# A transformer layer on one core: even paces for the MLP's filler products, and its readouts split between ScalarE and GpSimd

## Chip, cores and metric

The kernel runs on one core of one Trainium2 chip. The metric is the time of one execution on the device in microseconds (us); lower is better.

## What is computed

One layer in which attention and a dense MLP run in parallel on the same normalized input, in fp32 (2048 tokens, width 512, 32 heads of 16, 1792 hidden columns):

```python
xn = _layernorm(x, axis=-1)
return x + _A_ref(xn, A_wqkv, A_wo) + _B_ref(xn, B_w1, B_b1, B_w2, B_b2)

# _A_ref: q, k, v of xn @ wqkv, 32 heads
scores = jnp.einsum("bhqd,bhkd->bhqk", q, k) * (Dh ** -0.5)
p = _softmax(scores, axis=-1)
o = jnp.einsum("bhqk,bhkd->bhqd", p, v)        # then @ wo
# _B_ref
h = _gelu(jnp.einsum("bsd,df->bsf", x, w1) + b1)
return jnp.einsum("bsf,fd->bsd", h, w2) + b2
```

## The kernel before

**The sweep.** Attention is a sweep of 512 *units*. Four heads and 512 queries make a tile of 16 units; there are 32 tiles. In a unit TensorE makes four *S* products (scores laid out by query, into banks pS), of which VectorE takes the maxima (L259, `mt`); and, for the unit 20 earlier, four *E* products (scores laid out by key, with the maximum taken off, into banks pT), of which ScalarE makes the exponentials (L304, `pe`). Two *V* halves then multiply the exponentials by the values into the bank pV; they are in fp32, and TensorE makes each of them in two passes.

TensorE's array is used as two groups of 64 rows by four groups of 32 columns, so each product is four instructions (L169), one for each column group, and two products run side by side where one has the upper and one the lower rows. A unit has two halves, `a` = 0 and 1. In each *half unit* stand two S and two E products, then a V half on one row group, and beside it, on the other row group, the *filler* D.

**The filler.** `dense` puts products of the MLP (and of the projections, before and after it) beside the V half. They come from a list of `Group`s, each with one bank pD. A *first-layer group* (`hidden_group`) has 12 products for each row group and gives 128 hidden columns of 512 tokens; there are 56. A *second-layer group* (`sum_group`) has 21 products for each row group and gives 128 tokens; there are 32. How many products a half unit takes is the group's `pace`: a pair of which odd and even units take turns. Both kinds have (3, 4), projections (4, 4). Since a group ends only with a unit, a first-layer group takes 4 units (3, 4, 3 and 2 products a half unit) and a second-layer group 6 (3, 4, 3, 4, 3, 4). First-layer groups stand three, two and two between the second-layer groups of the block of tokens before.

**Readouts.** At the end of a group's last unit ScalarE reads its bank. For a first-layer group that is `hh` (L1005): an Identity with a scale and a bias that are columns, one number for each partition. From the next unit on GpSimd makes hh's cubic for the gelu (L983 to L985), then ScalarE the tanh (L972, `t`), then GpSimd the rest (L977 to L980, result `g`, which the second layer reads). For a second-layer group it is `yt` (L1031): a copy with a scale that is a column; GpSimd adds it to the running sum (L1033). Once in 16 units ScalarE also reads pV (L330, `osb`), and VectorE makes three small operations for the maxima (L270, L280, L281) and a reciprocal (L348).

**Order.** The order on each engine is the order in which the program is written: `unit` writes a unit, `later(n, ...)` puts a step n units on, `pooled` puts steps on GpSimd's list, which takes some 2500 ns of them a unit. pD and pT share four banks in turn: while a group holds one, the E products have three.

Of the kernel before, what the change touches and what calls it, by code (L numbers as in the profile page):

```python
# [10 lines left out]
I32 = mybir.dt.int32  # L11
# [36 lines left out]
def layer_kernel(ctx: ExitStack, tc: tile.TileContext, x, wqkv, wo, w1, b1, w2, b2, out):  # L48
# [110 lines left out]
    def given(engine, ns):  # L159
        backlog[engine] += ns  # L160
# [37 lines left out]
            product(user, dst[j:j + 32], lhs[:, j:j + 32], rhs, start=start, stop=stop)  # L198


    scale_reg, held = nc.scalar.alloc_register("exp_scale"), [None]

    def exp_scale(m):

        if held[0] != m:
            nc.scalar.reg_load(scale_reg, sexp[0:1, m:m + 1].bitcast(I32))
            held[0] = m
        return scale_reg

    mt_of, ptiles, pv_of = {}, {}, {}  # L210
    queue, slot = [], [0]
# [13 lines left out]
    def pooled(*todo):  # L225
        steps.extend(todo)
# [66 lines left out]
    def e_half(u, n):  # L293

        p, a = divmod(n, 2)
        t, kt = divmod(u, 16)
        g, qb = divmod(t, NQB)
        st = banks("T")
        r = slice(64 * a, 64 * a + 64)
        k0 = (kt % 4) * P  # L300
        tiled(None, st, kst[g % 2][p][kt // 4][r, k0:k0 + P], qst[g % 2][p][qb][r, :], True, True)
        pe = work.tile([P, QB], F32, name="pe", bufs=12)
        ptiles[u, n] = pe
        nc.scalar.activation(pe, st, AF.Exp, scale=exp_scale(g // 2))  # L304
        given("act", 470)

    def v_half(u, a):
# [107 lines left out]
    class Group:  # L415
# [3 lines left out]
        def __init__(self, prods, alloc, finish, ready=None, first=True, last=True, upper=None, pace=FAST):  # L419
            self.prods = prods, prods if upper is None else upper  # L420
            self.alloc, self.finish, self.ready = alloc, finish, ready
            self.first, self.last, self.pace = first, last, pace
            self.n, self.at, self.bank, self.key = [len(p) for p in self.prods], [0, 0], None, None

        def left(self, side=0):
            return self.n[side] - self.at[side]
# [1 line left out]
        def usable(self, side=0):  # L428
            return self.left(side) > 0 and (self.ready is None or self.ready(self.at[side]))

        def product(self, side):

            if self.bank is None:
                self.bank, self.key = self.alloc()
            lhs, rhs = self.prods[side % 2][self.at[side % 2]]()
            start = self.first and self.at == [0, 0]
            if side == 2:
                self.at = [min(self.at[0] + 1, n) for n in self.n]
                nc.tensor.matmul(self.bank, lhs, rhs, start=start, stop=self.last and self.over())  # L439
# [139 lines left out]
    def dense(gen, side):  # L579

        f = group(gen)
        for _ in range(0 if f is None else (f.pace if pos[0] <= NU + 1 else LATE)[pos[0] % 2]):
            if not f.usable(side):
                return
            f.product(side)

    def land():

# [373 lines left out]
    def mlp():  # L962
# [5 lines left out]
        def gelu(hh, g, b, f):  # L968
            t1 = m2.tile([P, QB], F32, name="t1", bufs=2)

            def tanh():
                nc.scalar.activation(t1, t1, AF.Tanh, scale=GELU_C * GELU_A)  # L972
                given("act", 600)
                later(1, rest, True)

            def rest():
                pooled((690, lambda: nc.gpsimd.tensor_scalar(t1, t1, 1.0, gs[:, 1:2], op0=ALU.add, op1=ALU.mult)),  # L977
                       (1280, lambda: nc.gpsimd.tensor_tensor(t1, t1, hh, op=ALU.mult)),  # L978
                       (620, lambda: nc.gpsimd.tensor_scalar(g[:, 0, f, :], t1, 1.0, 0.0, op0=ALU.mult, op1=ALU.add)),
                       (1160, lambda: nc.gpsimd.tensor_tensor(g[:, 1, f, :], t1, g[:, 0, f, :], op=ALU.subtract)),  # L980
                       (0, lambda: done.add((b, f))))
# [13 lines left out]
        def hidden_group(s, f):  # L995
# [6 lines left out]
            def hidden(hp):  # L1002
                hh = m2.tile([P, QB], F32, name="hh", bufs=3)
                scale, bias = fac1[0][:, k // 2:k // 2 + 1], b1_s[:, k:k + 1]
                nc.scalar.activation(hh, hp, AF.Identity, bias=bias, scale=scale)  # L1005
                given("act", 700)
                later(1, lambda: gelu(hh, g, s, f), True)

            return Group([lambda c=c, i=i, j=j: (wc[:, i, c, :], xb[:, j, c, :]) for c in range(NC) for i, j in PAIRS],
                         dbank, hidden, pace=MEAN)  # L1010

        def sum_group(s, q):
            b, t, g = s // 2, s // 2 * 4 + q, gts[s]
# [14 lines left out]

            def store(yp):
                yt = m2.tile([P, D], F32, name="yt", bufs=2)  # L1030
                nc.scalar.activation(yt, yp, AF.Copy, scale=gs[:, 2:3])  # L1031
# [159 lines left out]
```

## Time and profile before

| | |
|---|---|
| time, median of 3 runs | 1552.85 us (1550.26 to 1552.85) |
| the profiled execution | 1555.34 us, of which 1553.6 us are the span of its instructions |
| TensorE's granted clock, mean of the span | 0.993 of full speed; 1.00 from 600 to 1400 us |
| the sweep's middle | 600 to 1400 us: the MLP's groups follow one another without a pause |

In the page, PE is TensorE's matmuls, PEld its weight loads, DVE VectorE, ACT ScalarE, POOL GpSimd. A row of the groups gives line, engine and operation, written tile <- read tiles, shapes, count, then busy us, mean ns of one, and the idle time ahead with what ended it. ScalarE's operations overlap their neighbours a little, so the time for which one keeps the engine is read from its start to the start of the next.

### The profile page before, as it was taken

To read this page: it belongs to the slowest core of one execution; us is meant where nothing else is said; L and a number is where in the kernel's file an instruction comes from. 1 tells how busy PE (TensorE), PEld (TensorE's weight loads), DVE (VectorE), ACT (ScalarE), POOL (GpSimd) and SP (SyncE) were. 2 spreads that over 40 slices of the span, in tenths; PEclk is the share of its full clock that TensorE was granted. 3 is DMA by queue.
4 is the path that set the end of the run, shared out by engine and by line. 5 is a ranking of instruction groups with operands and counts; after the bars stand their busy time and mean duration, and the time that the engine had idled before them with its cause. 6 is when DMAs were issued, how large, how long until landed. Compare 5 with 4: busy or idle time off the path is not lost.

```text
span 1553.6 us, 86338 instructions
## 1 busy us (share of the span) xinstructions
PE 1514.5 (97%) x39203; PEld 806.0 (52%) x39203; DVE 1401.0 (90%) x2372; ACT 1251.6 (81%) x2326; POOL 674.6 (43%) x694
## 2 busy tenths in 40 slices
PE   8998999999999999999999999999999999999997
PEld 4434545555555555555555555555555555555443
DVE  7898989999999999999999999999999999999612
ACT  4316878889888888888888888888888888888771
POOL 3113697546465444435443443555254454521000
PEclk9999999999999999999999999999999999999997
DMA  6454576542111311121112111121112111022412
GB/s 210 124 158 142 167 231 197 180 120 88 50 35 47 91 33 34 36 75 42 35 56 65 46 35 35 35 80 55 36 42 60 45 35 35 22 66 60 150 50 86
DMA packets 113671, 123.72 MB, mean 80 GB/s; under 512 B 24988, under 2 KB 85276, under 8 KB 113304
## 3 DMA queue, kind: packets, MB, share of 16 engines
q1 hardware_dynamic: 113304, 118.21, 25.4%
q8 instruction: 306, 5.01, 1.4%
q14 instruction: 61, 0.50, 0.1%
HBM read 80.61 MB, written 37.34 MB: 76 GB/s over the span
## 4 chain that ended last, share of the span: by engine, by line
PE 84%; DVE 8%; ACT 2%; issue 2%; DMA 2%; SPq 1%; POOL 0%; ACTq 0%; POOLq 0%
PE pV L169 25%; PE pS L169 19%; PE pD L169 19%; PE pT L169 17%; DVE mt L259 6%; PE pT L439 1%; PE pS L439 1%; ACT pe L304 1%; ACT t L972 1%; DVE amx L667 1%; PE pT L532 1%; PE pD L439 1%; DMA ac<-acc_d 0%; PE pV L532 0%; SPq L1064 0%
## 5 line engine op out<-in xcount | busy, mean ns | idle before, releaser
L259 DVE TENSOR_REDUCE mt<-pS 128x1 f32<-128x512 f32 x2048 | 1299.9, 684 | 60.7 <-PE pS L169 43.1
L304 ACT ACTIVATE pe<-pT 128x512 f32<-128x512 f32 x2048 | 1100.0, 598 | 169.5 <-PE pS L169 72.3
L169 PE MATMUL pV<-pe,vv 64*32 64x512 f32 x8192 | 1077.6, 595 | 0.2
L169 PE MATMUL pT<-qst,kst 64*32 64x512 f16 x8192 | 708.2, 378 | 10.4 <-ACT pe L304 8.9
L169 PE MATMUL pS<-kst,qst 62*32 62x512 f16 x8192 | 636.8, 378 | 9.3 <-DVE mt L259 6.0
L169 PEld LDWEIGHTS <-qst 62*32 62x32 f16 x8192 | 271.1, 92 | 226.8 <-issue 77.9
L169 PEld LDWEIGHTS <-kst 64*32 64x32 f16 x8192 | 270.2, 91 | 213.7 <-issue 109.5
L169 PE MATMUL pD<-xb,wc 64*32 64x512 f16 x5376 | 370.5, 377 | 0.0
L169 PE MATMUL pD<-w_s,g 64*32 64x512 f16 x5376 | 359.4, 377 | 0.0
L169 PEld LDWEIGHTS pV<-pe,vv 64*32 64x32 f32 x8192 | 181.5, 105 | 111.2 <-PE pV L169 18.0
L983 POOL TENSOR_TENSOR t<-hh 128x512 f32<-128x512 f32 x56 | 58.3, 1042 | 341.2 <-ACT hh L1005 341.2
L169 PEld LDWEIGHTS <-g 64*32 64x32 f16 x5376 | 113.8, 92 | 38.6
L169 PE MATMUL pD<-xt,wqk_h 64*32 64x512 f16 x1920 | 127.6, 377 | 3.5 <-issue 3.5
L169 PEld LDWEIGHTS <-wc 64*32 64x32 f16 x5376 | 112.6, 91 | 31.1
L360 POOL TENSOR_TENSOR osb<-osb,rb 128x512 f32<-128x512 f32 x31 | 39.9, 1287 | 128.1 <-DMA rb<-den_d 95.1
L1033 POOL TENSOR_TENSOR xa<-xa,yt 128x512 f32<-128x512 f32 x32 | 41.0, 1280 | 119.0 <-ACT yt L1031 119.0
L1070 DVE SCALAR_TENSOR_TENSOR ac<-pS,gs,ac 128x512 f32<-128x512 f32 x20 | 15.0, 751 | 67.0 <-PE pT L169 46.9
L978 POOL TENSOR_TENSOR t<-t,hh 128x512 f32<-128x512 f32 x56 | 71.8, 1283 | 4.7
L985 POOL TENSOR_TENSOR t<-t,hh 128x512 f32<-128x512 f32 x56 | 71.7, 1280 | 4.7
L980 POOL TENSOR_TENSOR g<-t,g 128x512 f16<-128x512 f32 x56 | 65.3, 1166 | 4.7
L977 POOL TENSOR_SCALAR t<-t,gs 128x512 f32<-128x512 f32 x56 | 38.8, 693 | 55.5 <-ACT t L972 55.5
L169 PE MATMUL pS<-wo_s,oc 64*32 64x512 f16 x1008 | 61.7, 378 | 0.3
(139 smaller groups left out, 881.1 us busy)
## 6 DMA issues: line engine op xcount, KB each, us to landing
wch<-in_B_w_dram SPq DMA_DIRECT2D x28, 512.0 KB
wc<-w_d SPq DMA_DIRECT2D x56, 256.0 KB
qk_d<-stg SPq DMA_DIRECT2D x32, 256.0 KB
rb<-den_d SPq DMA_DIRECT2D x124, 64.0 KB
w_d<-wsp SPq DMA_DIRECT2D x28, 256.0 KB
kst<-qk_d SPq DMA_DIRECT2D x128, 48.0 KB
qst<-qk_d SPq DMA_DIRECT2D x128, 48.0 KB
xs<-in_A_x_dram SPq DMA_DIRECT2D x16, 256.0 KB
```

The costliest lines, as they stand in the source:

```text
L169: p = nc.tensor.matmul(*args, **kw)
L259: nc.vector.reduce_max(mt_of[t][:, n, qt, kb:kb + 1], s, axis=AX.X)
L304: nc.scalar.activation(pe, st, AF.Exp, scale=exp_scale(g // 2))
L360: pooled((1280, lambda: nc.gpsimd.tensor_tensor(osb, osb, rb, op=ALU.mult)), (620, lambda: nc.gpsimd.tensor_scalar(ot[:, 0], osb, 1.0, 0.0 ...
L439: nc.tensor.matmul(self.bank, lhs, rhs, start=start, stop=self.last and self.over())
L532: nc.tensor.matmul(pj, xt[:, i, c, t * P:(t + 1) * P], wh[j][:, c, :], start=(n == 0), stop=(n == 11))
L977: pooled((690, lambda: nc.gpsimd.tensor_scalar(t1, t1, 1.0, gs[:, 1:2], op0=ALU.add, op1=ALU.mult)), (1280, lambda: nc.gpsimd.tensor_tenso ...
L978: (1280, lambda: nc.gpsimd.tensor_tensor(t1, t1, hh, op=ALU.mult)),
L980: (1160, lambda: nc.gpsimd.tensor_tensor(g[:, 1, f, :], t1, g[:, 0, f, :], op=ALU.subtract)),
L983: pooled((1040, lambda: nc.gpsimd.tensor_tensor(t1, hh, hh, op=ALU.mult)), (620, lambda: nc.gpsimd.tensor_scalar(t1, t1, 1.0, 1.0 / GELU_A ...
L985: (1280, lambda: nc.gpsimd.tensor_tensor(t1, t1, hh, op=ALU.mult)),
L1033: add = lambda: nc.gpsimd.tensor_tensor(xa, xa, yt, op=ALU.add)
```

## The change

It has four parts.

1. A group counts in half products: `pace` is now a number of halves for each half unit, FAST (8, 8), MEAN (7, 7), SLOW (6, 6). First-layer groups go from MEAN to SLOW, three products in every half unit. Second-layer groups keep MEAN, now three and a half in every half unit; the half product is the product's first or last 256 of 512 columns (`part`), four instructions of their own with weights loaded again.
2. `hh` is read by a plain Copy; the scale and the bias move to a GpSimd step one unit later, ahead of the cubic.
3. `yt` takes its scale from a register that is loaded once, not from a column.
4. A tanh that is due when no group is open, or when 8 or fewer products of the open group are left (both row groups together), is put off by one unit.

ScalarE's order at the same place of the sweep, where two first-layer groups end one after the other (hh is a first-layer readout, t a tanh, pe an exponential, four of them a unit, yt a second-layer readout). Before:

```order
L1005 ACTIVATE hh<-pD,b_s,fac_2410 128x512
L304 ACTIVATE pe<-pT 128x512 x16
L1005 ACTIVATE hh<-pD,b_s,fac_2410 128x512
L972 ACTIVATE t_13028<-t_13028 128x512
L304 ACTIVATE pe<-pT 128x512 x16
L972 ACTIVATE t_13382<-t_13382 128x512
L304 ACTIVATE pe<-pT 128x512 x4
```

and after:

```order
L1016 ACTIVATE hh<-pD 128x512
L305 ACTIVATE pe<-pT 128x512 x16
L1016 ACTIVATE hh<-pD 128x512
L305 ACTIVATE pe<-pT 128x512 x4
L983 ACTIVATE t_13088<-t_13088 128x512
L305 ACTIVATE pe<-pT 128x512 x12
L983 ACTIVATE t_13451<-t_13451 128x512
L305 ACTIVATE pe<-pT 128x512 x4
```

The first tanh has moved from directly behind the second hh to four exponentials, one unit, later; the other one has kept its place.

TensorE's order in the first half unit of three and a half products of a second-layer group (w_s and g are the second layer's operands; the next rows are S and E products). Before, three products, each four pairs of a load and a matmul:

```order
L169 MATMUL pV<-pe,vv 32x512 x4
L169 LDWEIGHTS g
L169 MATMUL pD<-w_s,g 32x512
...
L169 LDWEIGHTS qst_1_2_111
L169 MATMUL pS<-kst_1_1_94,qst_1_2_111 32x512
```

and after, with four pairs more between the last whole product and the S product:

```order
L169 MATMUL pV<-pe,vv 32x512 x4
L169 LDWEIGHTS g
L169 MATMUL pD<-w_s,g 32x512
...
L169 LDWEIGHTS g
L169 MATMUL pD<-w_s,g 32x256
...
L169 LDWEIGHTS qst_1_2_111
L169 MATMUL pS<-kst_1_1_94,qst_1_2_111 32x512
```

TensorE has 64,224 rows in its order after and 62,688 before: 192 products (32 groups, two row groups, three each) are made in two parts.

GpSimd's order where the MLP's first chains begin. Before:

```order
L983 TENSOR_TENSOR t_8171<-hh 128x512
L984 TENSOR_SCALAR t_8171<-t_8171 128x512
L985 TENSOR_TENSOR t_8171<-t_8171,hh 128x512
L983 TENSOR_TENSOR t_8536<-hh 128x512
L984 TENSOR_SCALAR t_8536<-t_8536 128x512
L985 TENSOR_TENSOR t_8536<-t_8536,hh 128x512
L977 TENSOR_SCALAR t_8171<-t_8171,gs 128x512
```

and after:

```order
L1018 TENSOR_SCALAR hh<-hh,fac_2410,b_s 128x512
L994 TENSOR_TENSOR t_8172<-hh 128x512
L995 TENSOR_SCALAR t_8172<-t_8172 128x512
L996 TENSOR_TENSOR t_8172<-t_8172,hh 128x512
L1018 TENSOR_SCALAR hh<-hh,fac_2410,b_s 128x512
L994 TENSOR_TENSOR t_8538<-hh 128x512
L995 TENSOR_SCALAR t_8538<-t_8538 128x512
L996 TENSOR_TENSOR t_8538<-t_8538,hh 128x512
L988 TENSOR_SCALAR t_8172<-t_8172,gs 128x512
```

One step stands ahead of each cubic; the rest of the order is the same.

The diff, without the lines that only carry the new register or the new counters:

```diff
-FAST, MEAN, SLOW, LATE = (4, 4), (3, 4), (3, 3), (6, 6)
+FAST, MEAN, SLOW, LATE = (8, 8), (7, 7), (6, 6), (12, 12)
...
-        def product(self, side):
+        def product(self, side, parts=2):
...
             r = slice(64 * side, 64 * side + 64)
-            self.at[side] += 1
-            tiled("D", self.bank, lhs[r], rhs[r], start, self.last and self.over())
+            done = self.part[side]
+            n = min(parts, 2 - done)
+            cols = slice(done * QB // 2, (done + n) * QB // 2)
+            self.part[side] = (done + n) % 2
+            self.at[side] += (done + n) // 2
+            assert not start or n == 2
+            tiled("D", self.bank[:, cols], lhs[r], rhs[r][:, cols], start, self.last and self.over())
+            return n
...
-        for _ in range(0 if f is None else (f.pace if pos[0] <= NU + 1 else LATE)[pos[0] % 2]):
-            if not f.usable(side):
-                return
-            f.product(side)
+        n = 0 if f is None else (f.pace if pos[0] <= NU + 1 else LATE)[pos[0] % 2]
+        while n > 0 and f.usable(side):
+            n -= f.product(side, n)
...
-            def tanh():
+            def tanh(again=1):
+                if again and (cur[0] is None or cur[0].left(0) + cur[0].left(1) <= 8):
+                    later(1, lambda: tanh(0), True)
+                    return
                 nc.scalar.activation(t1, t1, AF.Tanh, scale=GELU_C * GELU_A)
...
-                nc.scalar.activation(hh, hp, AF.Identity, bias=bias, scale=scale)
-                given("act", 700)
-                later(1, lambda: gelu(hh, g, s, f), True)
+                nc.scalar.activation(hh, hp, AF.Copy)
+                given("act", 600)
+                later(1, lambda: pooled((690, lambda: nc.gpsimd.tensor_scalar(hh, hh, scale, bias, op0=ALU.mult, op1=ALU.add)),
+                                        (0, lambda: gelu(hh, g, s, f))), True)
...
-                         dbank, hidden, pace=MEAN)
+                         dbank, hidden, pace=SLOW)
...
-                nc.scalar.activation(yt, yp, AF.Copy, scale=gs[:, 2:3])
+                nc.scalar.activation(yt, yp, AF.Copy, scale=factor(sum_scale, gs[0:1, 2:3]))
```

More of the change, by code (lines that the diff above doesn't have):

```diff
@@ L198, in tiled, with factor @@
             product(user, dst[j:j + 32], lhs[:, j:j + 32], rhs, start=start, stop=stop)
[L201 to L208, printed above, removed]
+    exp_scale, sum_scale = (nc.scalar.alloc_register(n) for n in ("exp_scale", "sum_scale"))
+    held = {}
+    def factor(reg, src):
+        if held.get(reg.name) != str(src):
+            nc.scalar.reg_load(reg, src.bitcast(I32))
+            held[reg.name] = str(src)
+        return reg
     mt_of, ptiles, pv_of = {}, {}, {}
@@ L303, in e_half @@
         ptiles[u, n] = pe
-        nc.scalar.activation(pe, st, AF.Exp, scale=exp_scale(g // 2))
+        nc.scalar.activation(pe, st, AF.Exp, scale=factor(exp_scale, sexp[0:1, g // 2:g // 2 + 1]))
         given("act", 470)
```

8 lines of the change are left out of this document (5 added, 3 removed).

## Prediction

> **What bounds the kernel now.** I read the page first: busy time and the chain of waits, then the groups of instructions by shape.
>
> ```profile
> PE 1514.5 (97%) x39203; PEld 806.0 (52%) x39203; DVE 1401.0 (90%) x2372; ACT 1251.6 (81%) x2326; POOL 674.6 (43%) x694
> ...
> PE 84%; DVE 8%; ACT 2%; issue 2%; DMA 2%; SPq 1%; POOL 0%; ACTq 0%; POOLq 0%
> PE pV L169 25%; PE pS L169 19%; PE pD L169 19%; PE pT L169 17%; DVE mt L259 6%; PE pT L439 1%; PE pS L439 1%; ACT pe L304 1%; ACT t L972 1%; DVE amx L667 1%; PE pT L532 1%; PE pD L439 1%; DMA ac<-acc_d 0%; PE pV L532 0%; SPq L1064 0%
> ```
> ```profile
> 600.00:1400.00 800.00, 793.85 (x22220) 436.39 (x22212) 772.21 (x1273) 707.70 (x1319) 364.46 (x366) 1.00 0.16 46
> ```
> ```profile
> L304 ACT ACTIVATE pe<-pT 128x512 f32<-128x512 f32 x2048 | 1100.0, 598 | 169.5 <-PE pS L169 72.3 <-PE pT L169 70.3
> L1005 ACT ACTIVATE hh<-pD,b_s,fac 128x512 f32<-128x512 f32 x56 | 43.6, 778 | 3.9
> L506 ACT ACTIVATE pf<-pD 128x512 f32<-128x512 f32 x21 | 12.6, 599 | 10.9 <-PE pS L126 3.8 <-PE pS L169 3.1 <-PE pD L169 2.3
> ```
>
> TensorE is busy 97% of the span and 794 of the 800 us from 600 to 1400, and the chain runs over it for 84%; but VectorE has 772 of those 800 us and ScalarE 708. "Busy" therefore doesn't say what a unit of the sweep costs. For that I took the timelines of single engines and measured from one readout of the MLP's bank to the next. In a timeline each row is start (us), time (us), engine and operation, the count of merged instructions, and in brackets the idle time before. First ScalarE:
>
> ```profile
> 630.04 0.69 ACT L1031 ACTIVATE yt<-pD,gs 128x512 f32<-128x512 f32 x1
> ...
> 640.41 0.78 ACT L1005 ACTIVATE hh<-pD,b_s,fac 128x512 f32<-128x512 f32 x1
> 641.09 2.05 ACT L304 ACTIVATE pe<-pT 128x512 f32<-128x512 f32 x4
> ...
> 650.93 0.78 ACT L1005 ACTIVATE hh<-pD,b_s,fac 128x512 f32<-128x512 f32 x1
> 651.61 0.62 ACT L972 ACTIVATE t<-t 128x512 f32<-128x512 f32 x1
> 652.12 2.05 ACT L304 ACTIVATE pe<-pT 128x512 f32<-128x512 f32 x4
> ...
> 663.20 0.60 ACT L330 ACTIVATE osb<-pV 128x512 f32<-128x512 f32 x1
> 663.69 1.09 ACT L304 ACTIVATE pe<-pT 128x512 f32<-128x512 f32 x2
> ...
> 667.33 0.69 ACT L1031 ACTIVATE yt<-pD,gs 128x512 f32<-128x512 f32 x1
> 667.92 2.05 ACT L304 ACTIVATE pe<-pT 128x512 f32<-128x512 f32 x4
> ...
> 683.03 0.69 ACT L1031 ACTIVATE yt<-pD,gs 128x512 f32<-128x512 f32 x1
> ```
> ```profile
> 1121.83 0.78 ACT L1005 ACTIVATE hh<-pD,b_s,fac 128x512 f32<-128x512 f32 x1
> ...
> 1132.80 0.78 ACT L1005 ACTIVATE hh<-pD,b_s,fac 128x512 f32<-128x512 f32 x1
> ```
> ```profile
> 752.41 0.78 ACT L1005 ACTIVATE hh<-pD,b_s,fac 128x512 f32<-128x512 f32 x1
> 753.09 0.62 ACT L972 ACTIVATE t<-t 128x512 f32<-128x512 f32 x1
> ...
> 768.71 0.69 ACT L1031 ACTIVATE yt<-pD,gs 128x512 f32<-128x512 f32 x1
> ```
>
> A first-layer group lasts 4 units, a second-layer group 6, so the same 4 units take 10.37 us after a yt (630.04 to 640.41), 10.52 us after an hh (640.41 to 650.93) and 10.97 us after an hh with a tanh behind it (1121.83 to 1132.80). The same 6 units take 15.70 us after a yt (667.33 to 683.03) and 16.30 after hh and tanh (752.41 to 768.71). What differs is only how long ScalarE is kept from the next exponential: 0.59 us (667.33 to 667.92), 0.68 (640.41 to 641.09) and 1.19 (650.93 to 652.12). So each 0.1 us more of readout costs about 0.1 us of the program. The mechanism is seen at one such place, on all engines:
>
> ```profile
> 614.32 0.62 ACT L972 ACTIVATE t<-t 128x512 f32<-128x512 f32 x1
> ...
> 614.84 1.56 ACT L304 ACTIVATE pe<-pT 128x512 f32<-128x512 f32 x3
> 615.48 0.40 PE L169 MATMUL pT<-qst,kst 64*32 64x512 f16 x4 [0.39 <-ACT pe L304]
> ```
>
> The exponential that should free a bank of the scores begins at 614.84, and TensorE's next score product stands idle before 615.48 until that one is done. TensorE works in order there, so everything behind waits too.
>
> The second thing is the filler. TensorE's timeline in a second-layer group (each half unit has V's first pass, D's products, V's second pass, and the score products, left out here):
>
> ```profile
> 672.69 0.62 PE L169 MATMUL pV<-pe,vv 64*32 64x512 f32 x4
> 672.71 0.61 PE L169 MATMUL pD<-w_s,g 64*32 64x512 f16 x8
> 673.13 0.61 PE L169 MATMUL pV<-pe,vv 64*32 64x512 f32 x4
> 673.15 0.39 PE L169 MATMUL pD<-w_s,g 64*32 64x512 f16 x4
> ...
> 673.96 0.62 PE L169 MATMUL pV<-pe,vv 64*32 64x512 f32 x4
> ...
> 675.23 0.63 PE L169 MATMUL pV<-pe,vv 64*32 64x512 f32 x4
> 675.27 0.61 PE L169 MATMUL pD<-w_s,g 64*32 64x512 f16 x8
> 675.71 0.60 PE L169 MATMUL pD<-w_s,g 64*32 64x512 f16 x8
> ...
> 676.58 0.60 PE L169 MATMUL pV<-pe,vv 64*32 64x512 f32 x4
> ...
> 677.88 0.62 PE L169 MATMUL pV<-pe,vv 64*32 64x512 f32 x4
> ```
>
> From V to V, a half unit with three D products (8 + 4 instructions from 672.71) takes 1.27 us, and so does the next; with four (8 + 8 from 675.27) it takes 1.35 and then 1.30 (675.23, 676.58, 677.88). A unit of threes is 2.54 us, a unit of fours 2.65. With three, D's row group is free long before V's two passes (0.44 us apart) are, so V sets the length; with four, D and V end together and D sets it.
>
> **The change part by part.**
>
> (1) *Readouts.* hh loses its two per-partition operands, yt its one. Copies of the same shape without any take 0.599 us (pf), an exponential with its scale in a register 0.598 us. An osb, also such a copy, keeps ScalarE for 0.49 us (663.20 to 663.69). So I take 0.50 us in place of 0.68 and 0.59. The 56 scale-and-bias steps go to GpSimd, nearest row:
>
> ```profile
> L977 POOL TENSOR_SCALAR t<-t,gs 128x512 f32<-128x512 f32 x56 | 38.8, 693 | 55.5 <-ACT t L972 55.5
> ```
>
> at 0.7 us each that is 39 us on an engine with 364 busy us in 800. The chain behind hh grows by that step, and the second layer's products wait for its end; but the order has the same products in the same half units in both kernels, and a group's chain has four units for some 7 us of work. So I cost it at nothing; were the cover gone, it would be at most these 39 us. The register load for yt comes once.
>
> (2) *Tanh apart from hh.* Before, 27 of the 56 tanhs stand directly behind an hh; in the changed order one does, and the others stand four exponentials later. A tanh alone keeps ScalarE 0.51 us (651.61 to 652.12).
>
> (3) *What a readout costs.* 6 units of the second layer are by themselves 3 x 2.54 + 3 x 2.65 = 15.57 us, so behind a yt (0.59 us) 15.70 - 15.57 = 0.13 us is lost and behind hh and tanh (1.19 us) 16.30 - 15.57 = 0.73. The two agree: what exceeds 0.46 us is paid in full. By this an hh should cost 0.22 and its 4 units 0.09 more than behind a yt; they take 0.15 more. With 0.50 and 0.51 us, a readout then costs 0.04 and a lone tanh 0.05. Bounds: nothing, and the 0.13 of a yt for each.
>
> (4) *Paces.* First layer: 3, 4, 3, 2 products a half unit become 3, 3, 3, 3. The 4 units were 10.37 - 0.13 = 10.24 us by themselves and become 4 x 2.54 = 10.16; the short last unit had made good for the long second one, so little is gained. Second layer: 3, 3, 4, 4 become three and a half throughout. That is not in the trace. It lies between 2.54 us a unit (V still sets it) and 2.65 (it is as dear as four). In the rows above D is 0.216 us a product (a column group's stream restarts after that time; 675.27 to 675.71 holds two), so three and a half are 0.76 us against V's 2 x 0.44: V sets it, and I take 2.54. The half products are 256 columns wide, about 0.108 us, and the load of the next weights has to hide beneath:
>
> ```profile
> L169 PEld LDWEIGHTS <-g 64*32 64x32 f16 x5376 | 113.8, 92 | 38.6
> ```
>
> 0.092 us, which just fits.
>
> The sum, by groups (kinds counted on ScalarE's timeline of the whole run): a first-layer group becomes 10.16 + 0.04 + (after a first-layer one) 0.05, a second-layer group 6 x 2.54 + 0.04 = 15.28, or 15.33 with a tanh.
> First layer: 21 after a yt, 10.37 - 10.20 = 0.17, 3.6 us; 25 after an hh alone, 0.27, 6.8 us; 9 after hh and tanh, 0.72, 6.5 us; one after a projection, left out.
> Second layer: 10 after a yt, 0.42, 4.2 us; 4 after an hh alone, by (3) 15.57 + 0.22 + 0.05 - 15.33 = 0.51, 2.0 us; 18 after hh and tanh, 16.30 - 15.33 = 0.97, 17.5 us.
> Together 40.6 us. What lies ahead of the MLP and behind it is the same in order and count. The profiled execution took 1555.34 us and becomes 1514.7; the median of the runs, 1552.85, is 2.5 us below it, which gives **1512 us**.
>
> **Rivals.**
>
> *Instructions, not columns, set the half unit.* The half unit is 1.27 us with 12 D instructions and 1.32 on average with 16; three and a half products are again 16 instructions (12 of 512 columns and 4 of 256). If the count is what costs, every second-layer unit is 2.65: 32 x 6 x 0.11 = 21 us back, **1533 us**. For it: a half unit of threes leaves the D row group idle for 0.2 us and is still no shorter than V's 0.88 us and 0.39 more. Against it: in the rows above the instructions of one product start within hundredths of a us of one another. [...]
>
> *VectorE takes over.* Its reductions can run at
>
> ```profile
> 637.91 0.33 DVE L348 RECIPROCAL dn<-dn 64x32 f32<-64x32 f32 x1
> 638.17 4.84 DVE L259 TENSOR_REDUCE mt<-pS 128x1 f32<-128x512 f32 x8
> ```
>
> (the first of the 8 ends 0.68 us after its start, so (4.84 - 0.68) / 7 =) 0.594 us each, 2.38 us a unit. In every 16 units four small operations come in; the longest, the reciprocal dn, takes 0.26 us of its time (637.91 to 638.17), so the four take at most 0.07 a unit, and 2.45 in all. My groups average (56 x 10.24 + 32 x 15.32) / 416 = 2.56 us a unit, so 4% is left. But if the 2.54 us of the units of threes were already VectorE's own pace, the 0.07 would come on top: 2.61 us, 0.05 x 416 = 21 us back, **1533 us** as well. Against it: eight reductions in a row at 0.594.
>
> *The split costs.* If a half-wide piece held its row group as long as a whole one and its weights' load stood bare (0.216 + 0.092 us for each of four pieces), D would be 1.23 us and the half unit about 1.67 against 1.27: 384 of them, 154 us, **1666 us**, slower. It turns the sign from a half unit of 1.38 us on (41 us over 384). Against it: with whole products the load is hidden completely, and four products of 0.216 us fit in a half unit of 1.30.
>
> *The readouts don't get shorter or the collisions only move*: then only the pace is left, 32 x (15.57 - 15.24) = 11 us are won, **1542 us**. Against it: the plain copies (pf, osb) at 0.60 us, and the order.
>
> **How the numbers follow.** Forecast 0.66, instruction count 0.15, VectorE 0.10, collisions that only move 0.04, split costs 0.05. Low end: readouts and tanhs at no cost (88 x 0.04 + 56 x 0.05 = 6 us below 1512) and half units of 1.26 us, a hundredth less, in both layers (832 x 0.01 = 8 us), 1498. High end: the instruction count, 1533, and 0.09 us more at each of 88 readouts (the 0.13 of a yt in place of 0.04), 8 us: 1541. A measurement of this kernel can tell about 0.2%, 3 us, from no change. Faster by more than that are the forecast, the count, VectorE and most of the moved collisions, 0.92; within it 0.03, the rest of these where the paces bring nothing either; slower 0.05.
>
> **What would show it.** Right: hh and yt at about 0.60 us; 4 units from readout to readout at 10.2 to 10.3 us and 6 units at 15.3 to 15.4, whatever stood before; half units of 1.27 us in the second layer; the chain without "ACT t". Wrong: second-layer half units of 1.32 (count) or over 1.38 (split); units of 2.59 with VectorE's reductions end to end (VectorE); gaps ahead of score products that still end with an exponential.

## The result, and the profile after

| | before | after |
|---|---|---|
| time, median of 4 runs each | 1552.85 us | 1531.59 us (1529.93 to 1532.41) |
| ratio, with its 95% interval | | 0.9864 (0.9847 to 0.9881) |
| the profiled execution | 1555.34 us | 1531.77 us, span 1530.0 |
| granted clock, mean of the span | 0.993 | 0.993 |

The kernel became faster by 21 us; the forecast was 41, so about half of it came. The time lies in the range given, at its upper side: almost exactly where the rival "instructions, not columns, set the half unit" put it (1533).

The page of the kernel after: busy time, and the chain that ended last by engine and by line.

```profile
PE 1500.1 (98%) x39971; PEld 843.1 (55%) x39971; DVE 1398.2 (91%) x2372; ACT 1237.0 (81%) x2326; POOL 716.6 (47%) x750
...
PE 84%; DVE 10%; DMA 2%; issue 1%; ACT 1%; SPq 1%; POOL 0%; ACTq 0%; POOLq 0%
PE pV L169 25%; PE pS L169 19%; PE pT L169 18%; PE pD L169 17%; DVE mt L260 8%; PE pT L442 1%; PE pS L442 1%; DMA m_d<-mhl 1%; DVE amx L675 1%; PE pT L541 1%; PE pD L442 1%; PE pV L541 0%; DMA ac<-acc_d 0%; DMA xs<-in_A_x_dram 0%; SPq L1076 0%
```

The middle of the sweep, in the columns of the window shown for before (PE, PEld, DVE, ACT, POOL busy, then the granted clock):

```profile
600.00:1400.00 800.00, 798.74 (x23225) 471.12 (x23211) 782.98 (x1293) 708.26 (x1338) 392.43 (x403) 1.00 0.16 46
```

TensorE is as full as before and VectorE has gone from 772 to 783 of 800 us. From the chain's groups "ACT pe" and "ACT t", 1% each before, have gone; ScalarE as a whole has 1% of it, 2% before. The groups by shape:

```profile
L169 PE MATMUL pD<-w_s,g 64*32 64x256 f16 x1536 | 109.7, 273 | 0.0
L1018 POOL TENSOR_SCALAR hh<-hh,fac,b_s 128x512 f32<-128x512 f32 x56 | 43.0, 769 | 283.1 <-ACT hh L1016 283.1
...
L1016 ACT ACTIVATE hh<-pD 128x512 f32<-128x512 f32 x56 | 33.4, 597 | 5.6
L1043 ACT ACTIVATE yt<-pD 128x512 f32<-128x512 f32 x32 | 19.1, 597 | 3.8 <-PE pS L169 0.4 <-PE pD L169 0.3
```

Both readouts are plain copies of 0.597 us (778 and about 690 ns before), and the half-wide pieces are there, 1536 of them. GpSimd's new step costs 0.769 us, a little over the 0.7 taken, and nobody waits for GpSimd.

ScalarE's timeline, readout to readout:

```profile
656.01 0.60 ACT L1043 ACTIVATE yt<-pD 128x512 f32<-128x512 f32 x1
656.51 2.06 ACT L305 ACTIVATE pe<-pT 128x512 f32<-128x512 f32 x4
...
671.79 0.60 ACT L1043 ACTIVATE yt<-pD 128x512 f32<-128x512 f32 x1
...
682.05 0.60 ACT L1016 ACTIVATE hh<-pD 128x512 f32<-128x512 f32 x1
...
692.67 0.60 ACT L1016 ACTIVATE hh<-pD 128x512 f32<-128x512 f32 x1
```

A copy keeps ScalarE for 0.50 us (656.01 to 656.51), as taken. Four units after a yt take 10.26 us (671.79 to 682.05), six take 15.78 (656.01 to 671.79). The second number is the surprise: 15.28 was forecast, and it was 15.70 before. The four units behind the hh take 10.62 (682.05 to 692.67); this interval spans the change from one tile of 16 units to the next, and such intervals are some 0.3 us longer in both kernels (10.76 to 10.79 where 10.52 is usual before, 10.56 to 10.69 where 10.33 is usual after). Single intervals quoted below are from places without that change.

TensorE's timeline of second-layer half units at three and a half products:

```profile
657.37 0.61 PE L169 MATMUL pV<-pe,vv 64*32 64x512 f32 x4
...
658.00 0.28 PE L169 MATMUL pD<-w_s,g 64*32 64x256 f16 x4
...
658.67 0.63 PE L169 MATMUL pV<-pe,vv 64*32 64x512 f32 x4
...
659.81 0.37 PE L169 MATMUL pT<-qst,kst 64*32 64x512 f16 x1
659.99 0.62 PE L169 MATMUL pV<-pe,vv 64*32 64x512 f32 x3
...
661.30 0.63 PE L169 MATMUL pV<-pe,vv 64*32 64x512 f32 x4
```

From V to V it is 1.30, 1.32 and 1.31 us (657.37, 658.67, 659.99, 661.30), where 1.27 was taken: nearly what before had with four whole products (1.35 and 1.30). The pieces themselves are quick: they start at 658.00, and the whole half unit's D is over long before the V that starts at 658.67.

Added up over the run, from readout to readout on ScalarE's timeline (55 intervals that end with an hh, 31 that end with a yt, one of 8 units beside them):

| sum, us | first layer (55) | second layer (31) |
|---|---|---|
| before | 584.0 | 502.4 |
| after | 571.3 | 496.8 |
| won | 12.7 (16.9 forecast) | 5.6 (23.7 forecast, for 32) |

With the one long interval (0.6 us won) the groups gave 18.9 of the 23.6 us between the two profiled executions; 3.6 lie ahead of the first readout, in work that is the same in both, and 1.1 behind the last. The 3.6 us look like scatter: the same stretch takes anything from 314.7 to 319.3 us in the profiled executions of these kernels.

### The profile page after: what moved, and what is told of

The parts are those of the page before. It is cut to its first block, busy times and chain, and to the rows that moved or that the text cites. A ratio compares the mean times of both kernels' runs of the same rounds, so it can differ in the third digit from the quotient of the medians.

```text
span 1530.0 us, 87920 instructions
## 1 busy us (share of the span) xinstructions
PE 1500.1 (98%) x39971; PEld 843.1 (55%) x39971; DVE 1398.2 (91%) x2372; ACT 1237.0 (81%) x2326; POOL 716.6 (47%) x750
## 4 chain that ended last, share of the span: by engine, by line
PE 84%; DVE 10%; DMA 2%; issue 1%; ACT 1%; SPq 1%; POOL 0%; ACTq 0%; POOLq 0%
PE pV L169 25%; PE pS L169 19%; PE pT L169 18%; PE pD L169 17%; DVE mt L260 8%; PE pT L442 1%; PE pS L442 1%; DMA m_d<-mhl 1%; DVE amx L675 1%; PE pT L541 1%; PE pD L442 1%; PE pV L541 0%; DMA ac<-acc_d 0%; DMA xs<-in_A_x_dram 0%; SPq L1076 0%
## 5 line engine op out<-in xcount | busy, mean ns | idle before, releaser
L169 PE MATMUL pT<-qst,kst 64*32 64x512 f16 x8192 | 720.1, 378 | 4.6 <-DMA qst<-m_d 1.8
L169 PEld LDWEIGHTS <-qst 62*32 62x32 f16 x8192 | 284.2, 92 | 233.8 <-issue 107.3
L169 PE MATMUL pD<-w_s,g 64*32 64x512 f16 (+1 forms) x6144 | 360.9, 351 | 0.0
L169 PEld LDWEIGHTS <-kst 64*32 64x32 f16 x8192 | 277.4, 91 | 148.9 <-issue 55.8
L169 PEld LDWEIGHTS pV<-pe,vv 64*32 64x32 f32 x8192 | 177.0, 105 | 96.9 <-PE pS L169 9.8
L1018 POOL TENSOR_SCALAR hh<-hh,fac,b_s 128x512 f32<-128x512 f32 x56 | 43.0, 769 | 283.1 <-ACT hh L1016 283.1
L169 PEld LDWEIGHTS <-g 64*32 64x32 f16 x6144 | 132.5, 92 | 43.0 <-issue 0.8
```

What stands on the lines that cost most here:

```text
L169: p = nc.tensor.matmul(*args, **kw)
L1018: later(1, lambda: pooled((690, lambda: nc.gpsimd.tensor_scalar(hh, hh, scale, bias, op0=ALU.mult, op1=ALU.add)), (0, lambda: gelu(hh, g, ...
```

## The experiments

Theories. **Count:** a half unit's length grows with the number of its pairs of load and matmul, whatever they stream; so three and a half products, 16 pairs, cost what four do. **Stream:** the pieces cost time on D's row group, or stand where they delay the next products. **VectorE:** it has become the bound, so that shorter readouts show only in part. For the readouts there were the law (what keeps ScalarE longer than 0.46 us is paid in full) and its rival, that the collisions only move.

All ratios are to the kernel before, run beside it on the same chip, with 95% intervals. The sums are those of the table above.

| kernel | ratio | first layer | second layer |
|---|---|---|---|
| after | 0.9864 (0.9847 to 0.9881) | 571.3 | 496.8 |
| readouts_and_tanh | 0.9844 (0.9829 to 0.9859) | 573.3 | 490.7 |
| readouts_alone | 0.9895 (0.9878 to 0.9913) | 574.9 | 496.4 |
| tanh_alone | 0.9936 (0.9923 to 0.995) | 580.9 | 496.0 |
| paces_alone | 1.0008 (0.9993 to 1.0022) | 582.4 | 507.4 |
| no_split | 0.9831 (0.9817 to 0.9845) | 571.5 | 490.8 |
| count | 0.9898 (0.9875 to 0.9922) | 577.1 | 493.6 |
| d_first | 0.9875 (0.9858 to 0.9892) | 558.9 | 504.6 |
| mixed | 0.9762 (0.9743 to 0.9781) | 556.0 | 492.9 |
| short_first | 0.9718 (0.9699 to 0.9737) | 555.4 | 490.1 |

**The readouts and the tanh, without the paces.** The kernel after with the paces of before, in whole products:

```diff
-FAST, MEAN, SLOW, LATE = (8, 8), (7, 7), (6, 6), (12, 12)
+FAST, MEAN, SLOW, LATE = (8, 8), (6, 8), (6, 6), (12, 12)
...
-                         dbank, hidden, pace=SLOW)
+                         dbank, hidden, pace=MEAN)
```

> The changed kernel with the paces of before in both layers (3 and 4 whole products in turn), so that only the readouts (plain copies, scale and bias on GpSimd) and the tanh's place are changed. The prediction's sum without its paces: first layer 10.24 + 0.04 to 0.09, that is 10.3 us from readout to readout, second layer 15.57 + 0.04 to 0.09 = 15.6, whatever stood before; 1552.9 - 30 = about 1523 if every group were as undisturbed as the clean ones. Theory Q expects this to be faster than the changed kernel, about 1524 to 1528. If instead the changed paces win in the first layer what was not foreseen, it is slower than the changed kernel, over 1535.

Measured: 1532.58 us, 24 us less than before on that chip. Parts 2 to 4 give all of the gain. Whether the kernel is faster than the one after, as was expected, isn't shown, since the two intervals of the ratio overlap. Six units of the second layer take 15.61 us here, behind an hh as behind a yt.

**The readouts alone.** As above, and the tanh where it was:

```diff
-            def tanh(again=1):
-                if again and (cur[0] is None or cur[0].left(0) + cur[0].left(1) <= 8):
-                    later(1, lambda: tanh(0), True)
-                    return
+            def tanh():
```

> The kernel before with the plain copies alone (hh without scale and bias, which go to GpSimd; yt with its scale in a register); paces and the tanh's place as before. By the law of the prediction (what keeps ScalarE over 0.46 us is paid in full), hh and tanh together keep it 0.50 + 0.51 = 1.01 us, an hh alone and a yt 0.50: 27 x 0.18 + 29 x 0.18 + 32 x 0.09 = 13 us less than before, with groups behind hh and tanh still 0.5 us longer than the others. Rival: the tanh behind hh is what costs, and the copies' length does little, 3 us or less.

Measured: 1538.63 us, about 16 less, where 13 was expected. Part of the difference is that not only the readouts changed: the chain behind an hh is longer by GpSimd's new step, and so only 22 of the 56 tanhs stand directly behind an hh here, 27 before. Five collisions of 0.5 us are 2.5 us. ScalarE's timeline, with the collision still in it:

```profile
708.02 0.60 ACT L1013 ACTIVATE hh<-pD 128x512 f32<-128x512 f32 x1
708.52 0.62 ACT L980 ACTIVATE t<-t 128x512 f32<-128x512 f32 x1
...
724.14 0.60 ACT L1040 ACTIVATE yt<-pD 128x512 f32<-128x512 f32 x1
```

The six units behind hh and tanh take 16.12 us (708.02 to 724.14), 0.51 more than the 15.61 without a tanh: the length of the tanh (0.50 us to the copy, 0.51 for it), paid in full. The four units behind a lone hh fell from 10.52 to 10.27 (some take 10.34).

**The tanh alone.** The kernel before with part 4 only, the edit above turned round.

> The kernel before with part 4 of the change alone: a tanh that would stand directly behind an hh is put off by one unit. By the law (what keeps ScalarE longer than 0.46 us is paid in full) a place with hh and tanh, 1.19 us, becomes an hh of 0.68 us and a lone tanh of 0.51: 0.73 us of loss become 0.22 + 0.05, so 26 places give 26 x 0.46 = 12 us: 1555 becomes about 1543 (ratio 0.992), with 10.5 us from hh to hh everywhere and 15.8 us from hh to yt. Rival: a collision costs once, whatever its length (the readouts got shorter and that is what brought the gain, and the tanh's place is indifferent): no change, 1555, and the 10.97 us stay or move into the next unit.

Measured: 1545.18 us, 10 less; the law said 12. Hh to hh is 10.52 us now (median), also where 10.97 stood. The missing 2 us show on ScalarE's timeline:

```profile
660.62 0.69 ACT L1034 ACTIVATE yt<-pD,gs 128x512 f32<-128x512 f32 x1
661.21 0.62 ACT L975 ACTIVATE t<-t 128x512 f32<-128x512 f32 x1
...
676.84 0.69 ACT L1034 ACTIVATE yt<-pD,gs 128x512 f32<-128x512 f32 x1
```

Four of the 56 tanhs now stand directly behind a yt: two such intervals of six units take 16.22 us, as here (660.62 to 676.84), against 15.70, and two of four take 10.88 against 10.37. So four new collisions of some 0.5 us came where 27 went.

**The paces alone.** The kernel after with both readouts and the tanh as before.

> The kernel before with the changed paces alone (three products a half unit in the first layer, three and a half in the second, split by columns); readouts and tanh as before. The prediction's part (4) expects 32 x (15.57 - 15.24) = 11 us less than before and a little from the first layer. Theory Q (each pair of load and matmul lengthens a half unit, so three and a half products are as dear as four): second-layer groups 6 x 2.63 = 15.8 us by themselves in place of 15.57, 32 x 0.2 = 6 us more, the first layer even or up to 4 us less: 0 to 6 us more than before.

Measured: no difference, 1557.07 us against 1555.18. First-layer groups became 1.7 us shorter in sum, second-layer groups 5.0 longer: from yt to yt it is 15.87 us, where before had 15.78 (medians). The 11 us that the forecast gave to the second layer's paces aren't there; by these sums the sign is the other one.

**Whole products in the second layer.** The kernel after with three and four whole products in turn there, which takes the split out and leaves the rest:

```diff
-FAST, MEAN, SLOW, LATE = (8, 8), (7, 7), (6, 6), (12, 12)
+FAST, MEAN, SLOW, LATE = (8, 8), (6, 8), (6, 6), (12, 12)
```

> The changed kernel with the second layer's products whole again: three and four a half unit in turn, as before; first layer at three, readouts and tanh as changed. Theory Q (TensorE's lookahead counts instructions: three and a half products are 16 pairs of load and matmul, as many as four whole ones, so they are as dear): from readout to readout of a second-layer group 3 x 2.55 + 3 x 2.64 = 15.6 us in place of 15.78, 32 x 0.18 = 6 us less than the changed kernel's 1531.6, about 1526. Rival V (VectorE sets the pace of the changed kernel, not TensorE): nothing is won, 1531 to 1532. Rival S (the split does win what the paces promised, and something else took it back): 32 x 0.3 = 10 us more, about 1541.

Measured: 1529.92 us beside a before of 1556.75. The yt to yt interval:

```profile
792.53 0.60 ACT L1043 ACTIVATE yt<-pD 128x512 f32<-128x512 f32 x1
...
808.14 0.60 ACT L1043 ACTIVATE yt<-pD 128x512 f32<-128x512 f32 x1
```

is 15.61 us against 15.78 with the split, and the sum of the second layer 6.0 us less than after's. The split costs a little; it doesn't win.

**The number of pairs by itself.** In first-layer groups, one product in three has c of its four column groups cut in two pieces of 256 columns, c = 0 to 4 by the group's number. The columns streamed stay the same; the pairs go from 12 to 16 in a half unit.

```diff
...
+            if self.cut and self.at[side] % 3 == 2:
+                for j in range(0, P, 32):
+                    for c in ((slice(0, QB // 2), slice(QB // 2, QB)) if j < 32 * self.cut else (cols,)):
+                        product("D", self.bank[j:j + 32, c], lhs[r][:, j:j + 32], rhs[r][:, c], start=start, stop=stop)
...
-                         dbank, hidden, pace=SLOW)
+                         dbank, hidden, pace=SLOW, cut=(7 * s + f) % 5)
```

> The changed kernel, where in first-layer groups the middle one of the three products of each half unit has c of its four column groups made in two matmuls of 256 columns instead of one of 512; c is 0 to 4, by the group's number modulo 5. The columns streamed stay the same (three products, 0.65 us, 0.2 us shorter than V), the pairs of load and matmul are 12 + c. Theory Q: half units grow with c, flat at first and then up, from about 1.277 us on average (c = 0) to about 1.31 (c = 4, as with 16 pairs); mean over groups 0.015 us x 8 x 56 = 5 to 9 us over the changed kernel, about 1538. Rivals V and L, stream time: no growth with c, since D ends well ahead of V in all of them; 1531 to 1532.

Measured: 1542.56 us, 14 less than before on that chip and so a smaller gain than after's. Medians from V to V over all such half units (31 to 36 in each cell):

| pairs | 12 | 13 | 14 | 15 | 16 |
|---|---|---|---|---|---|
| first half unit, us | 1.290 | 1.297 | 1.306 | 1.314 | 1.322 |
| second half unit, us | 1.264 | 1.273 | 1.281 | 1.289 | 1.304 |

It is close to a straight line of 8 to 10 ns a pair, not flat at first as was expected, and at 16 it is at 1.322 and 1.304, the numbers of three and a half products (1.323 and 1.304, medians in after). A half unit of 13 pairs on TensorE's timeline:

```profile
680.30 0.63 PE L169 MATMUL pV<-pe,vv 64*32 64x512 f32 x4
...
680.75 0.61 PE L169 MATMUL pV<-pe,vv 64*32 64x512 f32 x4
680.77 0.38 PE L169 MATMUL pD<-xb,wc 64*32 64x512 f16 x4
...
681.40 0.40 PE L169 MATMUL pS<-kst,qst 62*32 62x512 f16 x4
681.60 0.62 PE L169 MATMUL pV<-pe,vv 64*32 64x512 f32 x4
```

and one of 16:

```profile
727.92 0.63 PE L169 MATMUL pV<-pe,vv 64*32 64x512 f32 x4
...
728.40 0.39 PE L169 MATMUL pD<-xb,wc 64*32 64x512 f16 x4
...
729.07 0.37 PE L169 MATMUL pT<-qst,kst 64*32 64x512 f16 x1
729.25 0.62 PE L169 MATMUL pV<-pe,vv 64*32 64x512 f32 x3
```

D's last four instructions start equally long after V in both, 0.47 and 0.48 us (680.30, 680.77; 727.92, 728.40), so the stream of the pieces costs nothing. What differs is the end. With 13 pairs the last four score products start together, 1.10 us behind V (681.40); with 16 they start one by one, the last 1.15 us behind V (729.07). The last score product ahead of V at 659.99 in after is such a single one too (659.81). What holds them up are their weight loads (PEld). First the half unit of 13 pairs:

```profile
681.37 0.10 PEld L169 LDWEIGHTS <-kst 64*32 64x32 f16 x3
681.58 0.14 PEld L169 LDWEIGHTS pV<-pe,vv 64*32 64x32 f32 x5
```

and one of 16 pairs, in after (V at 657.37):

```profile
658.43 0.10 PEld L169 LDWEIGHTS <-qst 62*32 62x32 f16 x2 [0.22 <-issue]
658.45 0.11 PEld L169 LDWEIGHTS <-kst 64*32 64x32 f16 x4
658.67 0.13 PEld L169 LDWEIGHTS pV<-pe,vv 64*32 64x32 f32 x5
```

Of the 16 score loads of a half unit some, three here and six there, start only when V's second pass is over (680.75 and 0.61 us, 681.37). They come some 8 ns apart, and the next V's loads start 0.2 us behind them. It is so in every half unit of the table whose 16 score loads are all in the trace: with 12, 13, 14, 15 and 16 pairs, 2, 3, 4, 5 and 6 score loads are late, and the next V's first load starts 0.19 us after the last late one (median in each cell). So each further pair of D makes one more score load late, and the next V with it; the time is lost behind D, not on D's stream.

**All D ahead of V.** The kernel after with the order of the two in a half unit changed for all groups:

```diff
-                if live and not new:
-                    v_half(w, r)
                 dense(gen, 1 - r)
-                if live and new:
+                if live:
                     v_half(w, r)
```

> The changed kernel with one thing turned round: in each half unit the filler's products are written ahead of the V half instead of behind it, so that they no longer stand between V's last pass and the next score products in TensorE's order. Same instructions, same operands. Theory Q: the score products of the next half come into the lookahead while V runs; half units of three and a half products fall from 1.31 to about 1.27 us, a second-layer group from 15.78 to about 15.3, 32 x 0.45 = 14 us less than the changed kernel, about 1517; first-layer half units about 1.27 as now. Rival V: VectorE sets the pace, nothing is won, 1530 to 1533. Rival L (the half pieces' own time or their weight loads are what costs): nothing is won either, half units stay at 1.31.

Measured: 1536.92 us, and what was expected for the second layer failed: it grew to 16.24 us from yt to yt. But the first layer shrank, to 10.02 us behind a yt. First the half units of 16 pairs, in the second layer:

```profile
796.11 0.63 PE L169 MATMUL pV<-pe,vv 64*32 64x512 f32 x4
...
797.43 0.39 PE L169 MATMUL pD<-w_s,g 64*32 64x512 f16 x4
797.46 0.63 PE L169 MATMUL pV<-pe,vv 64*32 64x512 f32 x4
```

V stands behind all of D's pairs in the order and starts only once D has started (797.43, 797.46); the half unit takes 1.35 us (796.11, 797.46). With 12 pairs, in the first layer:

```profile
771.99 0.64 PE L169 MATMUL pV<-pe,vv 64*32 64x512 f32 x4
772.04 0.72 PE L169 MATMUL pD<-xb,wc 64*32 64x512 f16 x8
...
773.18 0.74 PE L169 MATMUL pV<-pe,vv 64*32 64x512 f32 x4
...
774.45 0.64 PE L169 MATMUL pV<-pe,vv 64*32 64x512 f32 x4
```

V starts ahead of D, though it is written behind it (so in 400 of 448 half units of 12 pairs in the trace; with 16 pairs in the second layer in none), and the half units take 1.19 and 1.27 us (771.99, 773.18, 774.45). This can be read as the number of products in the half unit, or as something of the two kinds of group. The next two runs tell these apart.

**D first in the first layer only.** no_split, with D ahead of V in first-layer groups:

```diff
...
+                f = group(gen)
+                late = new or (f is not None and f.ahead)
-                if live and not new:
+                if live and not late:
                     v_half(w, r)
                 dense(gen, 1 - r)
-                if live and new:
+                if live and late:
                     v_half(w, r)
...
-                         dbank, hidden, pace=SLOW)
+                         dbank, hidden, pace=SLOW, ahead=True)
```

> Whole products in the second layer as in no_split, and in first-layer groups the filler written ahead of the V half as in d_first; readouts and tanh as changed. If the gain that the first-layer groups showed in d_first (10.02 in place of 10.27 us from readout to readout) and the second layer's of no_split (15.61 in place of 15.78) stand independently of one another: 56 x 0.25 = 14 us less than no_split, a ratio to before of about 0.974. Rival V (VectorE's 2.45 us a unit comes up next): first-layer groups stay at 10.0 to 10.1 but second-layer ones grow, ratio 0.978 to 0.983.

Measured: 1518.24 us, faster than both kernels. Four units behind a yt, on ScalarE's timeline:

```profile
666.63 0.60 ACT L1045 ACTIVATE yt<-pD 128x512 f32<-128x512 f32 x1
...
676.47 0.60 ACT L1018 ACTIVATE hh<-pD 128x512 f32<-128x512 f32 x1
```

9.84 us, 2.46 a unit, with the same operations on VectorE. So VectorE did not set after's 2.57 (10.26 / 4) or 2.63 us (15.78 / 6). The first layer's sum is 15.5 us below no_split's, where 14 was expected; the second layer's is 2.1 above it, with the same 15.61 us for six units, so VectorE takes back little if anything.

**D first wherever a half unit takes three products.** As mixed, but by the half unit, in both layers (`late` holds where the pace of this unit is 6 or less).

> The mixed kernel, but the order D before V now goes by the half unit and not by the kind of group: D stands ahead of V wherever a half unit takes three products (12 pairs of a load and a matmul), in second-layer groups too, and V ahead of D where it takes four. If the number of pairs decides (12 ahead of V leave V's loads in time, 14 to 16 do not), the six half units of three in a second-layer group lose the 0.03 to 0.06 us each that first-layer groups lost: 15.61 becomes 15.25 to 15.45 us and the time about 1507 to 1513 us, ratio to before 0.970 to 0.973. If it was the kind of group (its operands, its column groups), or if a change of order between one unit and the next costs as much as it gains, the second-layer groups stay at 15.6 us or grow: 1518 us or more, ratio 0.976 or above.

Measured: 1511.26 us. TensorE's timeline in a second-layer group, units of three and of four products in turn:

```profile
793.38 0.64 PE L169 MATMUL pV<-pe,vv 64*32 64x512 f32 x4
...
794.59 0.61 PE L169 MATMUL pV<-pe,vv 64*32 64x512 f32 x4
...
796.00 0.61 PE L169 MATMUL pV<-pe,vv 64*32 64x512 f32 x4
...
797.32 0.62 PE L169 MATMUL pV<-pe,vv 64*32 64x512 f32 x2
...
798.52 0.64 PE L169 MATMUL pV<-pe,vv 64*32 64x512 f32 x4
```

Half units of three, D first, take 1.20 to 1.21 us (793.38 to 794.59; 797.32 to 798.52), as in the first layer: so it goes by what the half unit holds and not by the kind of group (pairs and columns aren't told apart here: three products have fewer of both). But the half unit behind them, of four and V first, takes 1.41 (794.59 to 796.00) in place of mixed's 1.35, and the next 1.32 in place of 1.30. A change of the order between units gives most of the gain back: yt to yt is 15.51 us, not the 15.25 to 15.45 expected. So the time came out as expected, and the way to it did not. The second layer's sum is 2.8 us below mixed's, of 7 us between the medians; the two ran on different chips, and the profiled execution of mixed took 1512.83 us, of short_first 1513.60. That short_first is the faster of the two isn't shown. The chain by line shows what is next:

```profile
PE pV L169 21%; PE pD L169 20%; PE pS L169 18%; PE pT L169 15%; DVE mt L260 14%; PE pT L442 1%; PE pS L442 1%; DVE amx L677 1%; PE pT L541 1%; PE pD L442 1%; DMA m_d<-mhl 1%; SPq L1078 0%; PE pV L541 0%; DMA ac<-acc_d 0%; SPq L404 0%
```

VectorE's maxima have 14% of it (8% in after).

**Wider tiles.** no_split with D in matmuls of 64 columns instead of 32, half as many pairs (6 for three products):

```diff
-            tiled("D", self.bank[:, cols], lhs[r], rhs[r][:, cols], start, self.last and self.over())
+            stop = self.last and self.over()
+            for j in range(0, P, 64):
+                product("D", self.bank[j:j + 64, cols], lhs[r][:, j:j + 64], rhs[r][:, cols], start=start, stop=stop)
```

> no_split with each filler product beside a V half made in two matmuls of 64 columns of the array in place of four of 32: 6 pairs of load and matmul in place of 12 for three products, the same columns streamed. If it is the number of pairs that lengthens half units, by 8 ns each as in count, and matmuls of both widths run side by side: half units of threes 0.05 us shorter, first-layer groups 9.9 us, ratio to before about 0.965. If the array can't run both widths at once and has to drain between them, V and D come one after the other, half units of 1.9 us and more: 30% slower and over.

Measured: 2466 us in the fastest of four executions, 59% above before (1555.18 us on that chip). TensorE's timeline in a first-layer group:

```profile
900.32 1.03 PE L169 MATMUL pV<-pe,vv 64*32 64x512 f32 x8
901.27 0.83 PE L169 MATMUL pD<-xb,wc 64*64 64x512 f16 x6
...
902.49 1.02 PE L169 MATMUL pV<-pe,vv 64*32 64x512 f32 x8
```

D, in tiles of 64 by 64, starts only as V's second pass ends (901.27; V's rows end at 901.35), and the next V 1.22 us after D: side by side has become one after the other, 2.17 us a half unit. So it says nothing on the count of pairs. The half unit is as long as the expectation's second case has it (1.9 us and more); the trace shows that the two come one after the other, not why.

## Why the prediction came out as it did

**Right: what bounds the kernel, readouts and tanh, parts (1) to (3).** The copies take 0.597 us and keep ScalarE 0.50; the intervals hardly depend on what stood before them any more (10.27 and 10.33 us in first-layer groups, medians behind yt and hh; 15.78 and 15.77 in second-layer groups, at places without a change of tile); the chain has lost "ACT t". TensorE's score products stood idle for an exponential 22 times before, 8.9 us in all, and 3 times after, 1.4 us. The law held where it was taken apart: a tanh behind an hh costs its own length, 0.51 us. By the forecast's terms readouts and tanh were worth 40.6 less the paces (56 x 0.08 + 32 x 0.33 = 15), 26 us; alone they gave 24. Apart, the copies gave 16 where the law says 13, since five tanhs moved with them, and the tanh 10 where it says 12, for its four new collisions. GpSimd's 56 new steps, 43 us of busy time, cost nothing that shows.

**Wrong: part (4), the paces.** The step that failed reads "three and a half are 0.76 us against V's 2 x 0.44: V sets it, and I take 2.54". The unit is 1.323 + 1.304 = 2.63 us. That is 0.087 x 6 x 32 = 17 us. The first layer's threes are 2.554 us a unit in place of 2.54 (1.290 + 1.264 with 12 pairs), 4 x 0.014 = 0.06 a group, 3 us. Together they are 20 of the 21.7 us that the groups gave less than forecast (40.6 - 18.9). That the whole fell short by less is in part chance: 4.7 us came from outside the groups, where the forecast had nothing.

The fault is in how the comparison was made: the length of D's stream against the length of V's. The forecast saw that threes leave D's row group idle for 0.2 us, and took this for room. The count runs show that the room can't be used in that way: at the same number of columns each further pair lengthens the half unit by 8 to 10 ns, although D ends as early as ever, because one more weight load of the score products comes only behind V's second pass, and the next V behind it. With four whole products, too, it was hardly D's stream that set the length, as the forecast had it: in before six score loads are late there as well (in 140 of 174 half units of the second layer from 400 to 1400 us), and three products cut into 16 pairs take 2.63 us a unit, four whole ones 2.65. In before, units of three and of four whole products take 2.54 and 2.65 us, on average 2.60; at three and a half each, a unit takes 2.63. On a straight line by pairs the average of 12 and 16 is 14, and the split makes it 16 in every half unit. So the split lengthened what it was to shorten.

**The rivals.** *Instructions, not columns* is what happened; it was held at 0.15, and its price of 21 us was 4 too high since it took 2.65 us a unit for 2.63. The words "start within hundredths of a us of one another", set against it, were true of the D instructions and beside the point: the loss is on the score products' weight loads behind them. *VectorE takes over* named the same time and is refuted by mixed, with 2.46 us a unit for the same VectorE work. *The split costs* (1666 us) was far off, since the pieces' loads are hidden (D's last four instructions start 0.48 us behind V with 16 pairs, 0.47 with 13). *Collisions only move* is true of 4 of 56 tanhs in tanh_alone, 2 us, and no more.

**Open.** Where a pair's 8 to 10 ns go is shown: one more late weight load for each, 2 to 6 from 12 to 16 pairs. Why just these loads wait for the end of V's second pass isn't: that TensorE's lookahead counts instructions, as theory Q of the expectations has it, is an assumption of the author, and no run here separates it from a limit of another kind.

## What to carry to other kernels

Where two streams run side by side on TensorE, the idle time of the shorter one isn't yet room for more of it (here D's three products are 0.2 us shorter than V's two passes, 3 x 0.216 against 2 x 0.44, and each further pair still cost 8 to 10 ns): price an added product by its instructions as well as by its columns, in what it does to the start of the products behind it. A cheap test is to cut an operation into pieces without changing what it streams; the slope is the price of a pair of load and matmul (in count 1.290 to 1.322 us from 12 to 16), and it is known before the schedule is rebuilt. Where it isn't zero, look at which weight loads come late. An engine that is busy for 80% of the time can still set the length of single stretches: ScalarE had 81% in before, and there 4 units took 10.97 us behind an hh with a tanh, 10.52 behind an hh alone. Measure the intervals by what stood at their start, and pay out the difference.

## What was not expected of the hardware

- A pair of load and matmul that is hidden behind a longer stream costs 8 to 10 ns a half unit (in count 1.290 to 1.322 and 1.264 to 1.304 us from 12 to 16 pairs): one more weight load of the products behind it comes late (2 with 12 pairs, 6 with 16).
- The order in which two streams side by side are written is worth up to 4% in the first layer: with D's three products ahead of V, a group behind a yt falls from 10.27 to 9.84 us (after to mixed; 571.3 to 556.0 us over all 55, 3%), and with three and a half it costs 3% (15.78 to 16.24, after to d_first). In d_first TensorE started V's matmuls, on the other row group, ahead of D's where D's stand first in the order (771.99 and 772.04).
- Filler in tiles of 64 by 64 beside V in tiles of 64 by 32 hardly overlapped with it in wide (0.08 us, 901.27 to 901.35): 2.17 us a half unit.
- On 128x512 a Copy with its scale from a register took what a copy without any took (0.597 us, yt and hh in after), a Copy with a scale column 0.69 (yt in before), an Identity with a scale and a bias column 0.78 (hh in before): about 0.09 us for each column.
